# Loading q as 512-byte runs of two tokens, with the query order kept until the store

## The chip, the cores and the metric

The kernel runs on one core of one Trainium2 chip. The metric is the time of one execution in device microseconds (us). The profile of a core lists a tensor engine (PE, with its weight loads counted apart as PEld), a vector engine (DVE), a scalar engine (ACT), GpSimd (POOL) and a sync engine (SP) whose queue issues most transfers here (132 of 142 in the kernel before). It counts the busy share of DMA over sixteen engines, which move the data between device memory and the tiles on chip. The tiles of q, k and v and of the results have 128 partitions.

A run is put into a state, fast or slow; the slow one is a run more than 1.5% above the fastest of the same kernel. Ratios below use fast runs alone: the mean time of one kernel's fast runs over the mean of the other's of the same rounds, so they are not quite the ratio of the medians that stand beside them. Intervals are 95%.

## The reference, cut to what matters

Decayed linear attention in blocks, then a two-layer network on each token. Shapes: q, k, v are `[4, 8, 768, 64]` float32 (batch, head, token, element); the network is 512 to 2048 to 512; the output is `[3072, 512]`.

```python
for b in range(nb):                      # blocks of 64 tokens
    intra = einsum('bhic,bhjc->bhij', qb, kb) * Dmask
    intra = einsum('bhij,bhjd->bhid', intra, vb)
    inter = einsum('bhid,bhde->bhie', qb * lam_pow, kv_state)
    out[:, :, sl] = intra + inter
    kv_state = lam_block * kv_state + einsum('bhsd,bhse->bhde', kb * rev_pow, vb)
x = out.transpose(0, 2, 1, 3).reshape(B * S, H * D)
h = x @ w_in
g = where(h >= 1, h, where(h <= -1, 0, (h + 1) ** 2 / 4))
return g @ w_out
```

## The kernel before

The kernel works in 24 chunks of 128 tokens (C = 128). For each chunk it loads q, k and v, scales q and k by tables of powers of lam while casting to bf16, transposes them (by PE for chunks 0 to 5, by DMA after that), makes scores and the output of attention on PE, and copies that to `xT`. Four chunks form a group of 512 tokens for the two dense layers. A planner written in the kernel orders the instructions of every engine ahead of time.

A load puts one token on each partition. In memory one head of one token is 64 float32, so each contiguous run is 256 bytes. A store writes 128 token rows of 2,048 bytes:

```python
def f_load(c, x, wait):
    t = ld.tile([128, H, D], F32, name=f"x{x}f", tag=f"x{x}f")
    b, s0 = c // NCB, (c % NCB) * C
    d = nc.sync.dma_start(out=t, in_=(q, k, v)[x][b, :, s0:s0 + C, :].rearrange("h p d -> p h d"))
    # ... cut

def cast(c, x, eng):
    # ... cut
    eng.tensor_tensor(t, qkv_ld[c, x], _bc(tab[:, c % NCB, :], 2, D), op=AX.mult)

def f_s2(c):                             # scores, chunks 4 and up
    # ... cut
            nc.tensor.matmul(pst[c, hi][:, hp, :], lhsT=kT[c][HD[hi], hp, :], rhs=qT[c][HD[hi], hp, :],
                             start=True, stop=True)

def f_x(c):                              # attention output to the layers' input
    # ... cut
    nc.scalar.copy(out=xT[sx][:, :, off:off + C], in_=pot[c])

def f_st(s, ms):                         # s: group of 512 tokens, ms: 128 of them
    m0 = s * MS + ms * 128
    nc.sync.dma_start(out=out[m0:m0 + 128, :], in_=osb[s, ms])
```

## Time and profile before

The median before the change was 226.91 us (225.87 to 227.54, 3 runs).

| what | value | view |
|---|---|---|
| PE busy | 205.6 of 225.5 us | page, part 1 |
| PE waiting, all causes named | about 14 us, 7.8 of them for the first cast | waits of PE |
| q load, issue to landing | 4.4 us | DMA issues |
| store, issue to landing | 2.6 us | DMA issues |
| packets of 256 B (loads, transposes) | 92,160, median 18 ns | packet records |
| packets of 2,048 B (stores) | 3,072, median 85 ns | packet records |

These lines are from the page of the kernel before. A digit is the busy share of one fortieth of the span, in tenths; PEclk is the granted clock of PE.

```profile
span 225.5 us, 4385 instructions
PE 205.6 (91%) x1733; PEld 123.4 (55%) x1760; DVE 144.2 (64%) x218; ACT 123.6 (55%) x220; POOL 61.0 (27%) x65
...
PE   0497989999999989689999999999999999999992
...
PEclk9999999999999999999999999999999999999998
DMA  6999999999898797999999999999011001110212
```

PE is full from about slice 7 on, with small dips in slices 15 to 18. The DMA engines are full too, but only until slice 28 (157 us), where the last loads land. So PE is the limit, and the DMA engines are close behind it as long as loads run.

The view of waits says the same from the other side. Its columns are the waiting instruction, what it waited for, the total us, how often, and the longest.

```profile
PE pt L241 <- DVE ks L231: 7.8, 2, 7.5
PE pu L266 <- ACT vi L235: 2.3, 2, 1.7
PE ps L277 <- ACT qT L248: 1.7, 3, 0.8
```

The names are the program's own: `x0f`, `x1f`, `x2f` are the loaded q, k, v; `qs`, `ks`, `vi` their casts; `qT`, `kT` the transposed casts; `pt`, `ps` hold transposes by PE and scores, `pu` the update of the state, `po` the output of attention; `ph`, `py` are the two layers, `r` what ACT makes of `ph`, and `osb` the rows to be stored.

Two lines of the timeline of the kernel before show how much room a chunk has. The columns are start, duration, engine, source line and what is written from what.

```profile
85.95 1.19 SPq L260 DMA_TRANSPOSE qT<-qs  x1
...
88.41 0.21 PE L285 MATMUL ps<-qT,kT 64*128 64x128 bf16 x1
```

### The profile page before, as it was taken

The numbers are of one execution on the slowest core, as the hardware profiler recorded it, in microseconds if no ns is written. First come the engines' busy times: TensorE is split into PE (matmuls) and PEld (weight loads), VectorE is DVE, ScalarE is ACT, GpSimd is POOL, SyncE is SP. The second block draws the span as 40 slices with busy tenths as digits, with TensorE's granted clock in tenths as the row PEclk, the third lists the DMA queues.
The fourth block names the chain that finished last, engine by engine and source line by source line (L and its number), as shares of the span: only waits on it lengthen the run. The fifth ranks groups of instructions, "written<-read, shape, count | busy, mean of one in ns | idle before, by whom it ended". The sixth has DMA issues, their size and how long they took to land.

```text
span 225.5 us, 4385 instructions
## 1 busy us (share of the span) xinstructions
PE 205.6 (91%) x1733; PEld 123.4 (55%) x1760; DVE 144.2 (64%) x218; ACT 123.6 (55%) x220; POOL 61.0 (27%) x65
## 2 busy tenths in 40 slices
PE   0497989999999989689999999999999999999992
PEld 0376634765888577567664554545545544444441
DVE  7687399978498948567655956856656564554300
ACT  3346867544678285546757575676655444455121
POOL 6543560056034332423342542361000000000000
PEclk9999999999999999999999999999999999999998
DMA  6999999999898797999999999999011001110212
GB/s 121 216 218 170 195 189 202 200 223 196 212 202 158 182 215 169 205 173 204 225 196 237 214 166 233 232 211 211 0 49 47 24 22 49 47 47 16 77 67 77
DMA packets 102837, 34.38 MB, mean 152 GB/s; under 512 B 95136, under 2 KB 99744, under 8 KB 102816
## 3 DMA queue, kind: packets, MB, share of 16 engines
q1 hardware_dynamic: 97920, 29.90, 70.4%
q0 software_dynamic: 4752, 4.19, 12.2%
q8 instruction: 14, 0.23, 0.5%
q14 instruction: 7, 0.06, 0.1%
q10 hardware_dynamic: 144, 0.00, 0.0%
HBM read 27.27 MB, written 6.29 MB: 149 GB/s over the span
## 4 chain that ended last, share of the span: by engine, by line
PE 57%; SPq 3%; DMA 2%; issue 1%; ACT 1%; ACTq 0%
PE py L365 27%; PE ph L332 23%; PE po L305 3%; DMA x2f<-in_v_dram 2%; PE ps L285 2%; SPq L406 1%; PE po L302 1%; PE pu L266 1%; SPq L256 1%; SPq L260 1%; ACT vi L235 0%; ACT osb L370 0%; PE pt L285 0%; ACTq L370 0%
## 5 line engine op out<-in xcount | busy, mean ns | idle before, releaser
L332 PE MATMUL ph<-xT,w_in_sb 128*128 128x128 bf16 (+1 forms) x741 | 92.5, 268 | 1.9 <-ACT xT L312 1.0
L365 PE MATMUL py<-w_out_sb,gT 128*128 128x512 bf16 x368 | 92.6, 379 | 1.0 <-issue 0.2
L340 ACT ACTIVATE r<-ph,one 128x512 bf16<-128x512 f32 (+2 forms) x96 | 64.6, 678 | 47.7 <-PE ph L332 38.4
L332 PEld LDWEIGHTS <-w_in_sb 128*128 128x128 bf16 x752 | 52.5, 98 | 29.0 <-issue 2.2
L365 PEld LDWEIGHTS <-gT 128*128 128x128 bf16 x384 | 35.7, 98 | 38.8 <-DVE gT L356 0.2
L348 DVE TENSOR_SCALAR t<-r 128x1024 bf16<-128x1024 bf16 x48 | 25.2, 526 | 42.7 <-ACT r L340 42.7
L356 DVE TENSOR_TENSOR gT<-w,t 128x1024 bf16<-128x1024 bf16 x48 | 39.8, 828 | 1.6
L231 POOL TENSOR_TENSOR ks<-x1f,tab_k 128x512 bf16<-128x512 f32 x20 | 22.1, 1103 | 62.0 <-DMA x1f<-in_k_dram 48.9
L351 DVE TENSOR_TENSOR w<-r,t 128x1024 bf16<-128x1024 bf16 x48 | 37.2, 775 | 1.5
L231 POOL TENSOR_TENSOR qs<-x0f,tab_q 128x512 bf16<-128x512 f32 x24 | 28.5, 1189 | 25.7 <-DMA x0f<-in_q_dram 25.3
L235 ACT CAST vi<-x2f 128x512 bf16<-128x512 f32 x24 | 14.8, 616 | 16.5 <-DMA x2f<-in_v_dram 16.4
L295 DVE TENSOR_TENSOR sc<-ps,causal 128x512 bf16<-128x512 f32 x20 | 13.8, 689 | 13.6 <-PE pt L285 13.6
L370 ACT COPY osb<-py 128x512 f32<-128x512 f32 x24 | 14.1, 586 | 15.1 <-PE py L365 13.4
L305 PE MATMUL po<-sc,vi 128*128 128x128 bf16 x192 | 19.2, 226 | 0.2
L312 ACT CAST xT<-po 128x512 bf16<-128x512 f32 x24 | 14.0, 585 | 7.2 <-PE po L305 6.6
L270 ACT CAST ubd<-pu 64x256 bf16<-64x256 f32 x40 | 14.6, 364 | 5.3 <-PE pu L266 5.0
L305 PEld LDWEIGHTS <-vi 128*128 128x128 bf16 x192 | 15.2, 102 | 2.3 <-issue 0.6
L302 PE MATMUL po<-qT,ubd 128*128 128x128 bf16 x80 | 15.1, 224 | 0.0
L295 DVE TENSOR_TENSOR sc<-pt,causal 128x512 bf16<-128x512 f32 x20 | 13.6, 680 | 0.0
L266 PE MATMUL pu<-vi,ks 128*128 128x128 bf16 x80 | 8.4, 232 | 2.4 <-ACT vi L235 2.3
L241 PE MATMUL pt<-ident,ks 128*128 128x128 bf16 x24 | 3.1, 266 | 8.0 <-DVE ks L231 7.8
L266 PEld LDWEIGHTS <-ks 128*128 128x128 bf16 x80 | 6.4, 105 | 5.5 <-issue 3.1
(48 smaller groups left out, 87.4 us busy)
## 6 DMA issues: line engine op xcount, KB each, us to landing
x1f<-in_k_dram SPq DMA_DIRECT2D x24, 256.0 KB, 4.8
x0f<-in_q_dram SPq DMA_DIRECT2D x24, 256.0 KB, 4.4
x2f<-in_v_dram SPq DMA_DIRECT2D x24, 256.0 KB, 4.6
out_dram<-osb SPq DMA_DIRECT2D x24, 256.0 KB, 2.6
w_out_sb<-in_moe_w_out_dram POOLq DMA_DIRECT2D x4, 512.0 KB, 13.3
w_in_sb<-in_moe_w_in_dram POOLq DMA_DIRECT2D x3, 512.0 KB, 6.6
w_in_sb<-in_moe_w_in_dram POOLq DMA_DIRECT2D x2, 256.0 KB, 5.0
kT<-ks SPq DMA_TRANSPOSE x18, 4.2
```

The lines of the kernel that those rows point to most:

```text
L231: eng.tensor_tensor(t, qkv_ld[c, x], _bc(tab[:, c % NCB, :], 2, D), op=AX.mult)
L235: nc.scalar.copy(out=v_out(vi[c % NV]), in_=qkv_ld[c, 2].rearrange("p (a b) d -> p a b d", b=2))
L266: nc.tensor.matmul(pu[0][:, hp, :], lhsT=pair(ks[c], hp), rhs=v_pair(vi[c % NV], hp), start=(c % NCB == 0 and hp == 0), stop=True, skip_gr ...
L295: nc.vector.tensor_tensor(sc_sb[c][:, g], pst[c, g], _bc(causal, 1, HP), op=AX.mult)
L302: nc.tensor.matmul(po[:, hp], lhsT=ubd[(c - 1) % NUB][:, hp, :], rhs=qT[c][:, hp, :], start=True, stop=False)
L305: nc.tensor.matmul(po[:, hp], lhsT=vi[c % NV][:, hp, hi].rearrange("p a d -> p (a d)"), rhs=sc_sb[c][:, hi, hp, :], start=(cb == 0 and hi ...
L332: nc.tensor.matmul(ph[:, j * m:(j + 1) * m], lhsT=w_in_sb[:, ko, (ni + j) * 128:(ni + j + 1) * 128], rhs=xT[s][:, ko, part * m:(part + 1) ...
L340: nc.scalar.activation(out=r_t[grp][:, i, cs], in_=ph_t[s, ni, part][:, cs], func=AF.Relu, bias=one[:, 0:1])
L348: nc.vector.tensor_scalar(t_t[grp], r, 0.5, 1.0, op0=AX.mult, op1=AX.min)
L351: nc.vector.tensor_tensor(w_t[grp], r, t_t[grp], op=AX.subtract)
L356: nc.vector.tensor_tensor(gT[s][:, f - RW * n:f, part * m:(part + 1) * m], w_t[grp].rearrange("p a (b m) -> p (a b) m", m=m), t_t[grp].rea ...
L365: nc.tensor.matmul(py_t[s, ms], lhsT=gT[s][:, ko, ms * 128:(ms + 1) * 128], rhs=w_out_sb[:, ko, :], start=(ko == 0), stop=(ko == FO - 1))
```

## The change

The intent: two neighbouring tokens of one head lie next to each other in memory, so a load that takes them together has runs of 512 bytes and half as many packets (12,288 of 512 bytes instead of 24,576 of 256). To keep 128 partitions in use, heads 0 to 3 go to partitions 0 to 63 and heads 4 to 7 to partitions 64 to 127, each by a transfer of its own. The columns of a chunk's queries then stand in the order "even tokens, odd tokens". The change keeps that order through scores, attention and both layers, and undoes it only in the store, by writing partitions 0 to 63 to the even rows and 64 to 127 to the odd rows.

```diff
-    lam_b = const.tile([128, H], F32)
-    nc.scalar.dma_start(out=lam_b, in_=lam.partition_broadcast(128))
+    HL = H // 2
+    lam_b = const.tile([128, H + HL], F32)
+    nc.scalar.dma_start(out=lam_b[:, :H], in_=lam.partition_broadcast(128))
+    for g in range(2):
+        nc.scalar.dma_start(out=lam_b[64 * g:64 * g + 64, H:], in_=lam[g * HL:(g + 1) * HL].partition_broadcast(64))
     ... (two more iotas and two more table products for q; mask in the new query order)
@@ cast @@
+        if x == 0:
+            o = t.rearrange("p (e l) d -> p e l d", e=2)
+            i = i.rearrange("p (l e) d -> p e l d", e=2)
     ...
+    def q_cols(c, hp, rows=slice(0, 128)):
+        g, a = hp // 2, hp % 2
+        x = qT[c][rows, a, g * 64:(g + 1) * 64]
+        return bass.AP(x.tensor, x.offset, [list(x.ap)[0], [256, 2], [1, 64]])
     ... (the score and output matmuls read q_cols instead of qT)
@@ f_st @@
-        nc.sync.dma_start(out=out[m0:m0 + 128, :], in_=osb[s, ms])
+        nc.sync.dma_start(out=out[m0:m0 + 128, :].rearrange("(j e) n -> e j n", e=2), in_=osb[s, ms])
@@ f_load @@
-        d = nc.sync.dma_start(out=t, in_=(q, k, v)[x][b, :, s0:s0 + C, :].rearrange("h p d -> p h d"))
+        if x == 0:
+            for g in range(2):
+                i = q[b, g * HL:(g + 1) * HL, s0:s0 + C, :].rearrange("l (j e) d -> j l (e d)", e=2)
+                d = nc.sync.dma_start(out=t[64 * g:64 * g + 64].rearrange("p (l e) d -> p l (e d)", e=2), in_=i)
     ... (k and v as before; the planner's costs of a q load: 800 and 900 ns instead of 590 and 1190)
```

More of the change, by code (lines that the diff above doesn't have):

```diff
@@ L89 @@
     nc.scalar.preload_act_table_set("natural_log_exp_and_others")
-    lam_b = const.tile([128, H], F32)
-    nc.scalar.dma_start(out=lam_b, in_=lam.partition_broadcast(128))
+    HL = H // 2
[3 more added lines that the diff above has]
+        nc.scalar.dma_start(out=lam_b[64 * g:64 * g + 64, H:], in_=lam[g * HL:(g + 1) * HL].partition_broadcast(64))
     ident = const.tile([128, 128], BF16)
     make_identity(nc, ident)
-    ln_lam = const.tile([128, H], F32)
+    ln_lam = const.tile([128, H + HL], F32)
     nc.scalar.activation(out=ln_lam, in_=lam_b, func=AF.Ln)
-    pos_i = const.tile([128, NCB], I32)
-    nc.gpsimd.iota(pos_i, pattern=[[C, NCB]], base=-S // 2, channel_multiplier=1)
+    pos_i = const.tile([128, 3, NCB], I32)
+    nc.gpsimd.iota(pos_i[:, 0], pattern=[[C, NCB]], base=-S // 2, channel_multiplier=1)
+    for g in range(2):
+        nc.gpsimd.iota(pos_i[64 * g:64 * g + 64, 1:3], pattern=[[1, 2], [C, NCB]], base=-S // 2, channel_multiplier=2)
     causal = const.tile([128, 128], F32)
@@ L103 @@
         out=causal, in_=causal, compare_op=AX.is_ge, fill=0.0,
-        base=0, pattern=[[1, 128]], channel_multiplier=-1)
+        base=0, pattern=[[1, 2], [2, 64]], channel_multiplier=-1)
     NKB, NUB, NV = 3, 3, 4
@@ L112 @@
     nc.vector.memset(kbd[0], 0.0)
-    pos = const.tile([128, NCB], F32)
+    pos = const.tile([128, 3, NCB], F32)
     nc.vector.tensor_copy(pos, pos_i)
@@ L118 @@
         nc.gpsimd.memset(t, 0.0)
-    arg = const.tile([128, NCB, H], F32)
-    nc.vector.tensor_tensor(arg, _bc(pos, 2, H), _bc(ln_lam, 1, NCB), op=AX.mult)
+    arg = const.tile([128, NCB, 2, H], F32)
+    nc.vector.tensor_tensor(arg[:, :, 0], _bc(pos[:, 0], 2, H), _bc(ln_lam[:, :H], 1, NCB), op=AX.mult)
+    for e in range(2):
+        nc.vector.tensor_tensor(arg[:, :, 1, e * HL:(e + 1) * HL], _bc(pos[:, 1 + e], 2, HL),
+                                _bc(ln_lam[:, H:], 1, NCB), op=AX.mult)
+    tab_k = const.tile([128, NCB, H], F32)
+    nc.scalar.activation(out=tab_k, in_=arg[:, :, 0], func=AF.Exp, scale=-1.0)
     tab_q = const.tile([128, NCB, H], F32)
-    nc.scalar.activation(out=tab_q, in_=arg, func=AF.Exp)
-    tab_k = const.tile([128, NCB, H], F32)
-    nc.scalar.activation(out=tab_k, in_=arg, func=AF.Exp, scale=-1.0)
+    nc.scalar.activation(out=tab_q, in_=arg[:, :, 1], func=AF.Exp)
     for t in ubd + kbd[1:]:
@@ L230, in cast @@
         t = qkp.tile([128, H, D], BF16, name=nm, tag=nm)
-        eng.tensor_tensor(t, qkv_ld[c, x], _bc(tab[:, c % NCB, :], 2, D), op=AX.mult)
+        i = qkv_ld[c, x]
+        o, tb = t, _bc(tab[:, c % NCB, :], 2, D)
+        if x == 0:
+            o = t.rearrange("p (e l) d -> p e l d", e=2)
+            i = i.rearrange("p (l e) d -> p e l d", e=2)
+            tb = _bc(tab[:, c % NCB, :].rearrange("p (e l) -> p e l", e=2), 3, D)
+        eng.tensor_tensor(o, i, tb, op=AX.mult)
         d[c] = t
@@ L277, in f_s @@
                 nc.tensor.matmul(pst[c, g][:, 2 * hi + j, :], lhsT=kbd[c % NKB][:, 2 * g + j, hi, :],
-                                 rhs=qT[c][:, 2 * g + j, :], start=True, stop=True)
+                                 rhs=q_cols(c, 2 * g + j), start=True, stop=True)
     def f_s2(c):
@@ L284, in f_s2 @@
             for hi in range(2):
-                nc.tensor.matmul(pst[c, hi][:, hp, :], lhsT=kT[c][HD[hi], hp, :], rhs=qT[c][HD[hi], hp, :],
+                nc.tensor.matmul(pst[c, hi][:, hp, :], lhsT=kT[c][HD[hi], hp, :], rhs=q_cols(c, hp, HD[hi]),
                                  start=True, stop=True)
@@ L301, in f_o @@
             if cb > 0:
-                nc.tensor.matmul(po[:, hp], lhsT=ubd[(c - 1) % NUB][:, hp, :], rhs=qT[c][:, hp, :],
+                nc.tensor.matmul(po[:, hp], lhsT=ubd[(c - 1) % NUB][:, hp, :], rhs=q_cols(c, hp),
                                  start=True, stop=False)
@@ L405, in f_load @@
         b, s0 = c // NCB, (c % NCB) * C
-        d = nc.sync.dma_start(out=t, in_=(q, k, v)[x][b, :, s0:s0 + C, :].rearrange("h p d -> p h d"))
+        if x == 0:
+            for g in range(2):
+                i = q[b, g * HL:(g + 1) * HL, s0:s0 + C, :].rearrange("l (j e) d -> j l (e d)", e=2)
+                d = nc.sync.dma_start(out=t[64 * g:64 * g + 64].rearrange("p (l e) d -> p l (e d)", e=2), in_=i)
+        else:
+            d = nc.sync.dma_start(out=t, in_=(k, v)[x - 1][b, :, s0:s0 + C, :].rearrange("h p d -> p h d"))
         if wait is not None:
@@ L431 @@
         for x in (1, 0, 2):
-            add(("ld", it, x), "SP", 590, lambda i=it, x=x, wait=gated if x == 1 else None: f_load(i, x, wait),
-                [("cast", it - LD, x), ("w",) + w_seen[-2] if w_seen else None], due=pos_ * 1e-3, dma=1190)
+            add(("ld", it, x), "SP", 590 if x else 800, lambda i=it, x=x, wait=gated if x == 1 else None: f_load(i, x, wait),
+                [("cast", it - LD, x), ("w",) + w_seen[-2] if w_seen else None], due=pos_ * 1e-3, dma=1190 if x else 900)
             pos_ += 1
```

## The prediction

> **What bounds it now.** TensorE. The page gives PE 205.6 of 225.5 us (91%); in the stretches from 100 us on it is busy 19.8 of every 20 us, and the chain of waits is 57% PE. PE waits little: 7.8 us for the first cast, 2.3 us for v casts behind late loads (90 to 98 us). The DMA engines are second: nine tenths busy in almost every slice until the last loads land at 157 us, then nearly idle. The last chunk's transposes land about 17 us before PE reads them (175.7 us). So shorter loads buy at most some 3 us.
>
> **What the change costs and saves.**
> 1. Loads of q. The packet records show 92,160 packets of 256 B at a median of 18 ns (loads, transposes) and 3,072 of 2,048 B (stores) at 85 ns. A straight line through these puts 512 B near 28 ns, so a q load drops from 64 x 18 = 1.15 us per engine to 32 x 28 = 0.9 us (estimate). [...] I expect 0 to 6 us less DMA time in all, and one more issue on SP (0.6 us) per chunk.
> 2. Start: two more lam loads, two iotas and two table products before the first casts: about +1 us; at most -1 us from faster loads.
> 3. Matmuls read q columns as two runs of 64; casts read permuted q. Durations unchanged (PE 219 ns records, POOL 1,042 ns).
> 4. **Stores: the large term.** The output pattern becomes [2][64][512]. [...] Each store then puts 64 packets x 85 ns = 5.4 us on two engines instead of 8 x 85 = 0.7 us on sixteen.
>
> **On the critical path.** Twelve stores are issued before the last loads. They add 12 x 4.8 = 57 us to two engines which every load and transpose also needs; less about 8 us of DMA slack and q saving, the last load lands near 206 instead of 157 us. With 17 us of slack PE is about 33 us late. At the end four stores come 3.5 us apart but need 5.4 us each: the last lands some 9 us later. 226.9 + 33 + 9 - 1 = about 268 us.
>
> **Prediction:** 267 us, 8 in 10 between 243 and 290. Faster 0.02, same 0.07, slower 0.91.
>
> **What would show it.** Store landing: median from 2.6 to 6.5 us or more. Store packets unchanged (3,072 of 2 KB). Mean DMA share lower than now between 60 and 200 us, since fourteen engines wait for two. PE idle 30 us or more, released by casts, transposes or DMA; the last load near 200 us. q: 512 B packets, half as many (total down by 12,288). Matmul and cast durations as before.
>
> **What would make it wrong.** If the store still spreads over 16 engines, the rest is worth within 2 us either way: 224 to 229 us. If the two engines overlap store writes with load reads, the delay shrinks to perhaps 15 us. If SP waits on late stores with loads behind them, or PE's stalls slow its clock, it is worse than 290.

The sum is complete as it stands, 226.9 + 33 + 9 - 1 = 267.9 us, put on record as 267. But its 33 and 9 us rest on the two engines, which were the assumption at that time; the runs below test it.

## More of the kernel before

The transpose of one chunk's q is issued at 85.95 us and PE reads it at 88.41 us, 2.5 us later, without a wait. The same pair read off for all eighteen transposed chunks gives 2.5 to 6.1 us for chunks 6 to 18 and 9.8 to 19.9 us for the last five.

## The result and the profile after

The changed kernel took 294.82 us (294.35 to 295.22, 4 runs) against 227.22 us, a ratio of 1.2971 [1.2884, 1.3059]. It is slower by 30%, and it lies above the stated range of 243 to 290 us.

The page of the changed kernel, the same lines as before:

```profile
span 293.5 us, 4423 instructions
PE 218.9 (75%) x1733; PEld 130.0 (44%) x1760; DVE 138.6 (47%) x220; ACT 123.5 (42%) x220; POOL 59.0 (20%) x67
...
PE   0579899948189296759399739574999999999900
...
PEclk9999999986879789997789989976899999999975
DMA  6999999992697999979996667699911101111111
```

PE idles 74.6 us instead of 19.9 us (span less busy time). Its busy time grew by 13.3 us though the matmuls are the same, because the granted clock falls to half in stretches, 44 us in all before the tail (the low digits of PEclk). And the last two slices have no PE work at all.

The waits of PE in the changed kernel:

```profile
PE ps L305 <- DMA qT<-qs: 19.8, 5, 5.5
PE ph L352 <- ACT r L360: 10.0, 4, 4.6
PE pt L255 <- DVE ks L245: 9.7, 2, 9.3
PE pu L286 <- ACT vi L249: 8.9, 3, 7.0
PE ph L352 <- ACT xT L332: 5.5, 1, 5.5
```

The new waits are for transposes of q and for the cast of v, both behind DMA. The longest single wait after the start, 7.0 us, stands in the timeline of the changed kernel like this (in brackets the idle time before the row and what ended it):

```profile
73.82 0.44 PE L352 MATMUL ph<-xT,w_in_sb 128*128 128x128 bf16 x5
81.31 0.58 PE L286 MATMUL pu<-vi,ks 128*128 128x128 bf16 x4 [7.05 <-ACT vi L249]
```

The row of the whole tail, from the view of windows of the changed kernel (columns: stretch, its length, busy us of PE, PEld, DVE, ACT and POOL with their counts, granted clock, mean share of the 16 DMA engines, GB/s):

```profile
279.00:293.50 14.50, 0.00 (x0) 0.00 (x0) 0.00 (x0) 0.00 (x0) 0.00 (x0) 0.63 0.12 46
```

The same row of the kernel before, from the end of its last copy:

```profile
222.30:225.50 3.20, 0.00 (x0) 0.00 (x0) 0.00 (x0) 0.00 (x0) 0.00 (x0) 0.73 0.22 84
```

After the last result is copied, the changed kernel waits 14.5 us for stores alone, the kernel before 3.2 us. In that tail 0.12 of sixteen engines is busy, which is two engines (1.9), and they move 46 GB/s, or 23 GB/s each. The packet records say the same: in the changed kernel two packets of stores are in flight at a time in 131 of the 144 us that have any, and in the kernel before it is most often sixteen.

The last load is issued at 201.8 us instead of 152.5 us, 49 us later. From the timelines, before and after:

```profile
152.49 0.57 SPq L406 DMA_DIRECT2D x2f<-in_v_dram  x1
```

```profile
201.76 0.60 SPq L431 DMA_DIRECT2D x2f<-in_v_dram  x1
```

The prediction had 49 us. So its account of the DMA engines was right in the main; the step from there to PE was not. PE's last result is copied at 278.9 us instead of 222.2 us, 57 us later, where the prediction had 33.

Of the other signs, the late stores came: by the packet records the last packet of a store ends 7.7 us (median) after its issue, against 2.1 us before (the page gives no landing for these stores). One sign failed as it was written: the mean DMA share from 60 to 200 us rose from 0.81 to 0.95, since loads now run through all of that stretch. From 60 to 157 us, where both kernels load, it fell from 1.12 to 1.02, and the time with just two packets in flight rose from 0.9 to 8.9 us. (The share adds up the times of all packets, so it can exceed 1.)

### The profile page after: what moved, and what is told of

It reads as the page before. It is cut to its first block, busy times and chain, and to the rows that moved or that the text cites. A ratio compares the mean times of both kernels' runs of the same rounds, so it can differ in the third digit from the quotient of the medians.

```text
span 293.5 us, 4423 instructions
## 1 busy us (share of the span) xinstructions
PE 218.9 (75%) x1733; PEld 130.0 (44%) x1760; DVE 138.6 (47%) x220; ACT 123.5 (42%) x220; POOL 59.0 (20%) x67
## 5 line engine op out<-in xcount | busy, mean ns | idle before, releaser
L352 PE MATMUL ph<-xT,w_in_sb 128*128 128x128 bf16 (+1 forms) x743 | 101.4, 286 | 16.1 <-ACT r L360 10.0
L385 PE MATMUL py<-w_out_sb,gT 128*128 128x512 bf16 x366 | 97.9, 397 | 1.8 <-issue 1.3
L352 PEld LDWEIGHTS <-w_in_sb 128*128 128x128 bf16 x752 | 58.0, 105 | 47.8 <-issue 21.9
L368 DVE TENSOR_SCALAR t<-r 128x1024 bf16<-128x1024 bf16 x48 | 26.2, 545 | 68.6 <-ACT r L360 68.6
L385 PEld LDWEIGHTS <-gT 128*128 128x128 bf16 x384 | 37.2, 102 | 42.0 <-issue 6.3
L376 DVE TENSOR_TENSOR gT<-w,t 128x1024 bf16<-128x1024 bf16 x48 | 37.0, 770 | 1.5
L371 DVE TENSOR_TENSOR w<-r,t 128x1024 bf16<-128x1024 bf16 x48 | 36.2, 753 | 1.5
L245 POOL TENSOR_TENSOR qs<-x0f,tab_q 128x512 bf16<-128x512 f32 x24 | 25.9, 1079 | 44.7 <-DMA x0f<-in_q_dram 42.6
L305 PE MATMUL ps<-qT,kT 64*128 64x128 bf16 x80 | 8.4, 230 | 19.8 <-DMA qT<-qs 19.8
L305 PEld LDWEIGHTS <-kT 64*128 64x128 bf16 x160 | 5.1, 98 | 26.8 <-issue 15.3
L290 ACT CAST ubd<-pu 64x256 bf16<-64x256 f32 x40 | 14.5, 364 | 4.4 <-DVE kbd L258 2.2
```

What stands on the lines that cost most here:

```text
L245: eng.tensor_tensor(o, i, tb, op=AX.mult)
L290: nc.scalar.copy(out=ubd[c % NUB][HD[hi], :, HD[hi]], in_=pu[0][HD[hi], :, HD[hi]])
L352: nc.tensor.matmul(ph[:, j * m:(j + 1) * m], lhsT=w_in_sb[:, ko, (ni + j) * 128:(ni + j + 1) * 128], rhs=xT[s][:, ko, part * m:(part + 1) ...
L368: nc.vector.tensor_scalar(t_t[grp], r, 0.5, 1.0, op0=AX.mult, op1=AX.min)
L371: nc.vector.tensor_tensor(w_t[grp], r, t_t[grp], op=AX.subtract)
L376: nc.vector.tensor_tensor(gT[s][:, f - RW * n:f, part * m:(part + 1) * m], w_t[grp].rearrange("p a (b m) -> p (a b) m", m=m), t_t[grp].rea ...
```

## The experiments

Sixteen kernels ran after the prediction. The tables give medians of all runs, and ratios of fast runs to the kernel before of the same rounds. Some kernels give a wrong result, where that allowed one part to be changed alone; their bytes and their work stay the same. Kernels called "before" start from the kernel before, others from the changed one.

### The store alone, and the rest without it

Theory: the store on two engines causes the loss. Rival A: the q loads in halves do. Rival B: interleaved rows in memory are slow to write.

The first run keeps the change and splits each store in two, with 64 rows outermost in each:

```diff
-        nc.sync.dma_start(out=out[m0:m0 + 128, :].rearrange("(j e) n -> e j n", e=2), in_=osb[s, ms])
+        for e in range(2):
+            nc.sync.dma_start(out=out[m0:m0 + 128, :].rearrange("(j e) n -> e j n", e=2)[e], in_=osb[s, ms][64 * e:64 * e + 64])
```

> The changed kernel, but each store issued as two transfers, one for each partition half, each with 64 rows outermost; result correct. Theory (the store sits on two engines): the whole loss goes, 224 to 229 us; store landing back to 2 to 3 us; PE idle near 20 us. Rival A (the q loads in partition halves, or one more issue on the queue, starve PE): stays above 260 us. Rival B (rows of the result interleaved in memory make stores slow however they are split): stays above 260 us, tail above 8 us.

The next three take the kernel before and change only the store's row pattern, with 2, 4 or 16 outermost. The rows land permuted, so the result is wrong.

```diff
-        nc.sync.dma_start(out=out[m0:m0 + 128, :], in_=osb[s, ms])
+        nc.sync.dma_start(out=out[m0:m0 + 128, :].rearrange("(j e) n -> e j n", e=2), in_=osb[s, ms])   # or e=4, e=16
```

> The kernel before, with only the store's pattern changed to outermost 2 (rows land permuted, so the result is wrong on purpose). Theory: the store alone does it, 285 to 300 us, with stalls of PE and half-clock stretches as in the changed kernel, and a tail of about 14 us after the last result is copied. Rival A: about 227 us.

> As the run before, outermost size 4 (result wrong on purpose). Theory: 4 engines, 32 x 85 ns = 2.7 us each, so 12 x 2.0 = 24 us more on the busiest engines before the last load instead of 57, less 8 us of slack: 235 to 250 us; DMA share in the tail about 4/16. Rival B (interleaved rows): no better than with 2.

> As the run before, outermost size 16 (result wrong on purpose). Theory: 16 engines again, rows still far apart in memory: 225 to 229 us, the same as the kernel before. Rival B: clearly slower than the kernel before.

| kernel | median us | ratio |
|---|---|---|
| change, two stores (correct) | 246.36 | 1.0848 [1.0728, 1.0969] |
| before, store outermost 2 | 282.89 | 1.2443 [1.2337, 1.2549] |
| before, store outermost 4 | 263.10 | 1.1573 [1.1405, 1.1741] |
| before, store outermost 16 | 228.87 | 1.0080 [0.9984, 1.0175] |

The store alone costs 24%, at 282.89 us a little less than was expected. With 16 outermost the rows are at least as far apart in memory, and the time is 0.8% above the kernel before, which the interval does not separate from none, so Rival B falls: the loss goes with the outermost size, not with the order of the rows. (The run with 4 was made twice, the others four times.) But the first run did not come back to 227 us. Some 8% stays, which the theory had not expected and which Rival A alone would not explain either (it asked for 260 us or more).

The size-4 run was 13 us slower than the top of what was expected. Its 2,048-byte packets took 121 ns on average, a tenth of them 164 ns or more, instead of 95 ns on average. Why they took longer was not shown. An estimate from these packets, with the theory's four engines and so 32 packets on each instead of 8, is 12 stores of (32 x 121 - 8 x 95) ns = 3.1 us more each, or 37 us; in the run the last load was issued 33 us late and the last result copied 31 us late. (The run with 16 outermost has 121 ns on average too. Spread over sixteen engines, as the theory has it, a store puts only 8 packets on each there, and the run lost little.)

### The tail alone

The kernel before, with the two-engine store only for the last eight stores, when all loads are over (`s >= 4`; wrong):

```diff
+        o = out[m0:m0 + 128, :]
-        nc.sync.dma_start(out=out[m0:m0 + 128, :], in_=osb[s, ms])
+        nc.sync.dma_start(out=o.rearrange("(j e) n -> e j n", e=2) if s >= 4 else o, in_=osb[s, ms])
```

> The kernel before, with the two-engine store for the last eight stores only (result wrong on purpose): only the tail, after all loads. Theory: 226 plus 9 to 11 us, so 235 to 239 us, with no stalls of PE before the end and the clock at 1.00; the other 45 us of the loss of the store alone come from the stores that share the engines with loads.

It took 239.76 us against 227.79 us, 1.0514 [1.0457, 1.0571]: 12 us, just above what was expected. The view of windows of this run, its last stretch:

```profile
221.00:238.50 17.50, 2.19 (x11) 0.78 (x8) 0.00 (x0) 0.59 (x1) 0.00 (x0) 0.66 0.12 47
```

PE ends at about 223 us as before, and the rest is two engines (0.12 of sixteen) writing at 47 GB/s. By difference, 283 - 240 = 43 us of the store's loss come from the stores that are issued while loads still run.

### Does PE's half clock cost time?

In the kernel before with the outermost size 2, PE waited 25.9 us for transposes of q in eight waits, and its busy time was 11 us above that of the kernel before, because the clock fell to half in six stretches of 3.41 or 6.83 us before the tail. Four of them begin during or just after a wait for transposes of 3.4 to 5.5 us and one during a wait of 6.4 us for a copy to `xT`; the four shorter waits for transposes, 1.1 to 3.1 us, have none. The sixth, from 73.4 us, follows a wait of only 1.6 us. So in this run five of six falls of the clock go with a wait of 3.4 to 6.4 us; what sets the clock the traces do not show. One of these waits in that run, from its timeline; the matmuls after it take 0.31 us instead of 0.22:

```profile
128.08 1.03 PE L365 MATMUL py<-w_out_sb,gT 128*128 128x512 bf16 x4
134.64 0.26 PE L285 MATMUL ps<-qT,kT 64*128 64x128 bf16 x1 [5.53 <-DMA qT<-qs]
...
134.80 0.31 PE L285 MATMUL ps<-qT,kT 64*128 64x128 bf16 x1
```

The question is whether these 11 us are part of the loss or only fill time in which PE would wait anyway. The run puts 81 useless matmuls, 17.5 us of work, in front of the eight places:

```diff
+        for _ in range({6: 5, 7: 12, 10: 12, 11: 8, 13: 12, 14: 12, 16: 8, 17: 12}.get(c, 0)):
+            nc.tensor.matmul(pst[c, 0].rearrange("p a q -> p (a q)"), lhsT=w_in_sb[:, 0, 0:128], rhs=w_in_sb[:, 0, 0:512],
+                             start=True, stop=True)
```

> The kernel before with the two-engine store (283 us, result wrong on purpose) and 81 useless 512-column matmuls (17.5 us at full clock) put in front of the score matmuls of the eight chunks at which PE stalled in that run. If the half-clock stretches cost time (11 us more PE busy there): PE idles less, the clock stays near 1.00 before the tail and the time falls to 270 to 278 us. If the two engines set the pace and the clock is only a symptom: the fillers are absorbed by the stalls and the time stays at 280 to 286 us with a higher clock. If PE sets the pace after all: up to 300 us.

It took 283.67 us, 1.2467 [1.2385, 1.2549] of the kernel before, which is not clearly different from the run without the fillers (282.89 us, 1.2443). The lines of part 1 of the two pages, first without and then with the fillers:

```profile
PE 216.7 (77%) x1733; PEld 129.9 (46%) x1760; DVE 143.9 (51%) x218; ACT 123.5 (44%) x220; POOL 59.1 (21%) x65
```

```profile
PE 229.0 (81%) x1812; PEld 134.3 (48%) x1841; DVE 146.8 (52%) x218; ACT 122.7 (43%) x220; POOL 59.7 (21%) x65
```

PE did 12.3 us more in the same time. So PE is not what sets the pace while loads and stores share the engines; work of that size, put where PE stalls, is free there. The clock did not come back fully (half-clock time before the tail fell from 27.3 to 20.5 us), so the run does not show a kernel with the stalls and a full clock. It does show that PE had more time to spare than the half clock took.

### Another queue for the store

A store stands in SP's queue with the loads and the transposes behind it, and SP's timeline shows one issue after another (103 between 42 and 153 us in the kernel before, none overlapping). If that order were the trouble, another queue should help. The outermost size 2 again, issued from ACT (wrong):

```diff
-        nc.sync.dma_start(out=out[m0:m0 + 128, :].rearrange("(j e) n -> e j n", e=2), in_=osb[s, ms])
+        nc.scalar.dma_start(out=out[m0:m0 + 128, :].rearrange("(j e) n -> e j n", e=2), in_=osb[s, ms])
```

> The kernel before with the two-engine store issued from ScalarE's queue instead of SyncE's (result wrong on purpose): the same packets on the same two engines, but loads and transposes no longer stand behind a store in one queue. If PE's stalls are mostly transposes queued behind a store in order: stalls get shorter than 5.5 us and the time falls from 283 to 255 to 270 us. If it is the throughput of the two engines alone: 278 to 288 us, as before.

It took 289.31 us, 1.2794 [1.2750, 1.2838], worse than from SP and just above what the throughput theory allowed. PE's waits for transposes fell to 3.4 us, but its waits for ACT's results rose to 21.1 us. The lines of the waits, first with the store on SP, then on ACT:

```profile
PE ps L285 <- DMA qT<-qs: 25.9, 8, 5.5
```

```profile
PE ph L332 <- ACT r L340: 21.1, 5, 6.2
...
PE ps L285 <- DMA qT<-qs: 3.4, 1, 3.4
```

The waiting changed its place and hardly its sum (PE idles 63.5 instead of 65.4 us). The time alone decides nothing, because ACT itself was now stopped: in front of its stores it waited 44 us in all, up to 8.8 us at once, and the view names an earlier transfer, nearly always one of SP's, as what ended the wait. One such stop, from ACT's timeline:

```profile
58.16 0.69 ACT L340 ACTIVATE r<-ph,one 128x512 bf16<-128x512 f32 x1 [1.03 <-PE ph L332]
67.69 0.52 ACTq L374 DMA_DIRECT2D out_dram<-osb  x1
68.26 1.27 ACT L340 ACTIVATE r<-ph,one 128x512 bf16<-128x512 f32 x2 [9.42 <-DMA qT<-qs]
```

SP's own instructions tell the two theories apart. The table sums, from the timelines, how long SP took to issue the same 91 loads and transposes, from 42 us or so to the last load (a wait for another engine stands before an instruction here and is not in its length):

| kernel (from before) | SP issuing, us | last load issued, us | last result copied, us |
|---|---|---|---|
| before | 93.8 | 152.5 | 222.2 |
| store outermost 2, last eight only | 94.5 | 154.8 | 223.9 |
| store outermost 4, from SP | 124.4 | 185.7 | 253.5 |
| store outermost 2, from SP | 139.7 | 199.4 | 267.4 |
| store outermost 2, from ACT | 137.3 | 192.9 | 272.2 |

With two engines the same issues take 46 us longer on SP, about as much as the last load is late (47 us). They take 44 us longer too when no store stands in SP's queue at all. So the order behind a store is not the main cause: the loads and transposes are held up by what the two engines have to move, whichever queue the stores come from. Why a single issue lasts longer (a transpose up to 5.4 us instead of 2.5) the traces do not say.

### What the q load costs without the store

Here the change keeps its q load, and the copy to `xT` puts the queries back in order, so that the store of before can be used. The result is correct.

```diff
-        nc.scalar.copy(out=xT[sx][:, :, off:off + C], in_=pot[c])
+        nc.scalar.copy(out=xT[sx][:, :, off:off + C].rearrange("p k (j e) -> p k e j", e=2),
+                       in_=pot[c].rearrange("p k (e j) -> p k e j", e=2))
     (and the store of the kernel before)
```

> The changed kernel, but the copy from PSUM to xT puts the queries back in natural order, so that the store is the one transfer of before (128 rows outermost, 16 engines); result correct. What is left of the change is the q load in partition halves with 512-byte runs, one more issue per chunk and the strided reads. Theory (the extra 18 us of the run with two stores came half from the second q issue and half from the second store issue, on an in-order queue busy without a break, with no gain from the longer runs): 230 to 238 us. Rival (the split stores alone cost it): 225 to 229 us. Rival (the q halves alone cost it): 243 us or more.

It took 238.01 us, 1.0458 [1.0412, 1.0504]. The prediction had put all this within 2 us. The run with two stores took 246.36 us, so some 8 us of its loss belong to the split of the stores. To split the q side, the kernel before was given one part at a time. First, the same 256-byte load in two transfers of four heads, on all 128 partitions (correct):

```diff
+            for g in range(2):
+                hs = slice(g * H // 2, (g + 1) * H // 2)
+                d = nc.sync.dma_start(out=t[:, hs], in_=q[b, hs, s0:s0 + C, :].rearrange("h p d -> p h d"))
```

> The kernel before, with each q load issued as two transfers of four heads each, all 128 partitions and 256-byte runs as before; result correct. It adds the second issue alone (0.6 us per chunk on the queue)[...]. Issue theory: about the same loss as the run with q halves and the natural store, 230 to 238 us. Rival (the 64-partition halves are what costs): 226 to 229 us.

Then come 512-byte runs on all 128 partitions in one transfer, which reads the wrong tokens but as many bytes; and the same in two transfers, by heads or by partition halves. The last one tests whether it costs time to put a transfer on 64 of the partitions:

```diff
+            s2 = min(s0, S - 2 * C)
+            i = q[b, 0:H // 2, s2:s2 + 2 * C, :].rearrange("l (j e) d -> j l (e d)", e=2)
+            d = nc.sync.dma_start(out=t.rearrange("p (l e) d -> p l (e d)", e=2), in_=i)
     (by heads:  out=o[:, 2 * g:2 * g + 2], in_=i[:, 2 * g:2 * g + 2] for g in 0, 1)
     (by halves: out=o[64 * g:64 * g + 64], in_=i[64 * g:64 * g + 64] for g in 0, 1)
```

> The kernel before, with each q load reading 512-byte runs of two tokens of four heads onto all 128 partitions in one transfer (wrong data, so the result is wrong on purpose; the bytes and the rest are the same). The intent of the change without its costs. If runs of 512 bytes are worth what the fit of the packet records says: packets near 27 ns on average, 0.25 us less per q load, and 223 to 227 us, since PE is the limit. In partition halves the same packets took 37 ns on average.

> The kernel with 512-byte runs on all 128 partitions (wrong data on purpose), its q load issued as two transfers of two runs per partition each, still 128 partitions. It adds the second issue alone: about 1.5 us above that kernel's 224 us, as the heads split added to the kernel before: 225 to 227 us.

> The same, but the two transfers are the partition halves, as in the change (wrong data on purpose). [...]clearly slower than the heads split, 230 to 235 us, with more of the 512-byte packets above 37 ns. Rival (the rest of the 10 us was the table setup, the copy to xT in natural order and the second issue): equal to the heads split, 225 to 227 us.

| kernel (from before) | median us | ratio | 512-byte packets of 37 ns or more |
|---|---|---|---|
| 256-byte runs, two transfers by heads | 229.25 | 1.0097 [1.0031, 1.0163] | none of 512 B |
| 512-byte runs, one transfer, 128 partitions | 223.95 | 0.9845 [0.9807, 0.9882] | 13.1% |
| 512-byte runs, two transfers by heads | 227.23 | 1.0003 [0.9887, 1.0119] | 12.6% |
| 512-byte runs, two transfers by halves | 231.17 | 1.0233 [1.0154, 1.0312] | 27.5% |

The intent of the change is sound by itself: 512-byte runs gain 1.5%, near the 3 us that the prediction allowed for loads. A second transfer per load, whose issue takes SP 0.6 us (median, q loads of the kernel before), loses 1.0% (256 B) or about 1.6% (512 B), much less than the 230 to 238 us which the issue theory had expected of the first run. Putting the two transfers on partition halves loses another 2.3%. The last two figures are each uncertain by about one per cent, by the intervals; the 1.6% also compares runs of different rounds. The expectation that the packets of the full load would average 27 ns failed: the median is 27 ns everywhere, but the mean of the one-transfer run was 37.6 ns, as in the halves of the change (37.7 with the natural store), because a few packets are very long, up to 2.2 us. So the mean does not tell the two apart; the share of slow packets does. It doubles with halves, from 13.1% or 12.6% to 27.5%; why, the records do not show. By the medians, packets of 256, 512 and 2,048 bytes (18, 27 and 84 to 85 ns) move 14, 19 and 24 GB/s each; the last are of stores, so part of the difference may be the direction.

The second cost of halves shows best on the split stores of the first run, which had 64 partitions each: their 2,048-byte packets took a median of 154 ns instead of 85. The line of that run's DMA issues (size of one transfer, median us from issue to landing):

```profile
out_dram<-osb SPq DMA_DIRECT2D x48, 128.0 KB, 2.4
```

A half store takes 2.4 us to land; a whole one took 2.6 us before. Nothing is saved by halving, and there are twice as many.

Two small suspects were tried on the kernel before: the change's table setup (correct) and the strided copy to `xT` (wrong).

```diff
     (setup: the three lam loads, three iotas and three products of the change; q still uses its table of before)
     (copy: the two-line edit of f_x shown above, nothing else)
```

> The kernel before with the tables set up as in the change (three lam loads, three iotas, three products), q otherwise untouched; result correct. The first cast starts about 1.8 us later in the changed kernel. Theory: 1.5 to 2.5 us slower than before, about 229.5 us. Rival (absorbed by the rest of the start): within 0.7 us.

> The kernel before with the copy to xT written in two-column strides, as in the run with the natural store (result wrong on purpose: columns permuted). The copy took 735 instead of 585 ns there, 24 times 0.15 us. Theory: 1 to 3 us slower. Rival (ScalarE has time to spare): within 0.7 us.

The setup gave 1.0059 [0.9973, 1.0145] on two fast runs, a cost that the interval does not separate from none. The copy gave 0.9988 [0.9914, 1.0062], so ScalarE had time to spare for it. In the changed kernel's profile the first cast of k starts at 8.6 us instead of 6.8, and the cause can be read off: the logarithm of lam waits for three small loads until 6.2 us instead of one until 3.9 us.

The halves run explains 2.3% of the 4.6% against the kernel before, and the setup perhaps 0.6%. About 1.7% stays open. The permuted cast on POOL (median 1,108 ns instead of 1,042 with the natural store, but 1,042 in the changed kernel), the strided reads of PE, and the planner's different order, which follows from its new costs, were not separated.

### Can the gain of 512-byte runs be had?

Two correct kernels tried it. One load of q serves two chunks: 128 token pairs of 256 tokens on 128 partitions, 512-byte runs, one transfer on 16 engines; the copy to `xT` restores the order and the store stays as before. The second kernel does so only from chunk 4 on, so that the start stays as it was.

```diff
+            t = ldq.tile([128, H, 2, D], F32, name="x0f", tag="x0f")
+            d = nc.sync.dma_start(out=t.rearrange("p h e d -> p h (e d)"),
+                                  in_=q[b, :, s0:s0 + 2 * C, :].rearrange("h (j e) d -> j h (e d)", e=2))
     (the score of an even chunk now needs the q casts and transposes of two chunks;
      second kernel: only for c >= 4)
```

> A correct kernel with the intent of the change: one q load for two chunks, 128 partitions, 512-byte runs (token pairs of 256 tokens on the partitions), queries back in natural order in the copy to xT, stores as before. Against the kernel before: up to 3.8 us gained by the loads, some lost at the start (the first chunk waits for 512 KB of q and two casts, about 2 us) and 0.15 us per copy: 223 to 229 us; a gain above 2% is not expected.

> A correct kernel that should beat both: the first four chunks as in the kernel before, later q loads one for two chunks onto 128 partitions in 512-byte runs, queries put back in order in the copy to xT, stores as before. The start is that of the kernel before, so the 4 us lost by the version with two chunks throughout come back: 224 to 227 us, against 227.5 us before.

They took 231.65 us, 1.0224 [1.0173, 1.0275], and 230.96 us, 1.0196 [1.0128, 1.0264]. Both beat the changed kernel, neither the kernel before. In the first, PE does 25.7 us of work in the first 40 us instead of 28.9, partly at half clock, and that is most of its loss. In the second it still does only 26.8 us there, so the claim that the start would be unchanged failed. Where its time went exactly was not followed further. The 1.5% stays a gain that was shown only with wrong data.

## Why the prediction was wrong

The direction and the main cause were right; the size was too small by 28 us. Point by point:

1. "5.4 us on two engines", right, though its ground was not shown. The tail ran at 0.12 of sixteen engines, and the loss fell step by step with 2, 4 and 16 outermost (283, 263, 229 us).
2. "The last load lands near 206 instead of 157 us", right, though in part by luck. The last load was issued at 201.8 instead of 152.5 us. With the store alone it was issued at 199.4 us, 47 us late. But the prediction's 8 us of relief contained a saving of the q loads, and this did not come: with the q side alone the last load was issued at 158.2 us, later and not earlier.
3. "With 17 us of slack PE is about 33 us late", the first step that failed. With the store alone the last load is 47 us late and PE's last result is copied 45 us late (267.4 instead of 222.2 us), so nearly the whole delay reached PE and almost nothing was taken off for slack; in the changed kernel PE is 57 us late. The 17 us were read from the last chunk. But until chunk 18 the transposes are issued only 2.5 to 6.1 us before PE reads them, while they need 3.2 us (median) to land. So the schedule has hardly any slack while stores and loads compete. The room at the end comes afterwards and was not spent: the last transpose is issued 19.9 us before its use in the kernel before, 18.1 us with the store alone and 26.7 us in the changed kernel.
4. "The last lands some 9 us later": 12 us in the run that has only the tail, and 11 us in the changed kernel (14.5 less 3.2).
5. "The rest is worth within 2 us either way", the second step that failed. The q side costs 4.6% or 10 us by itself. The prediction named a second issue on SP (0.6 us) and halves on 64 partitions, but counted both as no gain and not as a loss. On a queue and on DMA engines that are full until 157 us (between 42.5 us and its last load SP issues for some 101 of 110 us), they are a loss: 1.0 to 1.6% for the second transfer and 2.3% for the halves, against 1.5% gained by the longer runs. The three together are the 2.3% of the halves run, half of the 4.6%; the rest was traced only in part.
6. "PE's stalls slow its clock" was named as a risk, and the clock did fall to half. But 17.5 us of extra PE work left the time unchanged, so the clock is a sign of the stalls here and not shown to be a cause of the loss.

The parts multiply to the whole: 1.2443 for the store and 1.0458 for the q side give 1.301; the change measured 1.2971 [1.2884, 1.3059].

## What to carry to other kernels

Before changing the shape of a transfer, look at the outermost size of both sides and test how many engines it leaves. Here an outermost size of 2 instead of 128, with the same bytes and packets, left two of sixteen (0.12 busy in the tail), and a store's last packet ended 7.7 us after its issue instead of 2.1. The loads and transposes were then held up, from whichever queue the stores were issued: with the store alone changed, SP took 46 us longer for the same 91 loads and transposes with the stores on its own queue, and 44 us longer with the stores on ACT's. When a delay in one resource is set against slack, take the slack from the tightest place in the stage where the delay arises, not from the end of the run. A split that looks neutral, such as two transfers for one or two halves of the partitions, was a cost here (1.0 to 1.6% for the second transfer, 2.3% for the halves), on a queue and on DMA engines with no free time.
